# Two groups of loads change queues in a backward recurrence, and the weight-gradient stage loads one tile per transfer

## The chip, the cores and the metric

The kernel runs on one core of one Trainium2 chip. The metric is the time of one execution on the device in microseconds (us). The kernel before took 4817.9 us, the median of three runs (4813.3 to 4832.0 us).

A core has a tensor engine (PE; its weight loads are listed as PEld), a vector engine (DVE), a scalar engine (ACT), GpSimd (POOL) and SyncE (SP), which here does nothing but issue transfers. Each engine works through its own list of instructions in order and waits on semaphores. Transfers between the chip's memory (HBM) and the core's on-chip memory are issued by SyncE, GpSimd or ACT, each on a queue of its own.

## What is computed

A block of a model, forward and backward. `xn` is the layer norm of `x` (2048 rows of 640). Part A is a recurrent attention: the rows go through 64 segments of 32 in order, each joined with 8 memory rows that the segment before it left:

```python
for s in range(n_seg):
    h = concatenate([mem, xs])                 # 8 memory rows and 32 rows of the segment
    q, k, v = h @ Wq, h @ Wk, h @ Wv           # 32 heads of 128
    p = softmax(mask(q @ k.T * scale))
    o = (p @ v) @ Wo
    mem, out[s] = o[:8], o[8:]
```

Part B is a gated feed-forward layer, `g = silu(B(xn))`, and the result is `x + A(xn) * g`. The outputs are this result and the gradients of `x`, of the first memory and of all seven weights. So the 64 segments are gone through a second time, from last to first, with the gradient of the memory rows.

## The kernel before

The program runs in stages: layer norm and the feed-forward layer (0 to about 250 us), first projections, the forward recurrence (to about 1590 us), the rest of attention and the prologue of the backward pass (to 1819 us), the backward recurrence (to about 3086 us), the gradients of Wq, Wk, Wv (to about 4240 us), and the rest. In the two recurrences and the weight gradients the order in which each engine does its work is the order in which the code is written: `in_order` (line 283) chains each engine's instructions.

**Backward recurrence** (`phase4_Abwd`, lines 1105 to 1572). A step of `chain(t, gap)` handles one segment's memory rows. It projects the gradient with Wo (L316), copies the two halves out (DVE and ACT, L90 and L92), turns them (L324), forms the value gradients (`vgrad`, L1214), the probability gradients, and sends everything back through Wv, Wk and Wq (L335) to the gradient that the next step starts from (L344, L360, L1352). Into the gaps between these (`gap("W0")` to `gap("G6")`) fall the *units*: the 32 rows of three segments at a time (a tile `tl` of 96 rows and 24 memory rows), four heads at a time (`qd`). A step takes two or three. A unit is loaded (`ld`, L1358), turned (`turn`, L1388 and L1395; its turned values go to HBM as VTD), multiplied (`dprob`, L1405), put through the softmax's gradient (`dsoft`; stored as DSA), and closed by `gmem` (L1433), whose result `gks` goes to HBM as GXP. There are four buffers for loaded units; the load of a unit follows the `gmem` of the one that frees its buffer. `gks` has one buffer.

Besides the units' loads a step needs loads of its own for the step after it. `load_g(t)` (line 1196) brings what the riding value gradients need, the 32 ordinary rows of the segment that ride along in `vgrad`: the output gradients `xr` (256 KB, tile named `gor` in the profile), the probabilities `prf` (256 KB, from PRA, also `gor`) and the memory rows' probabilities `prm` (80 KB, from PMX). It is written right after the step's `vgrad`, whose operands it overwrites. `prx_copy` (line 1204) then arranges `prf` on GpSimd for the next step's `vgrad`. Other loads are `loads` (VTD, PM), `load_q`, `load_k` (KS and rows, L1227 to L1234) and `load_xp`.

All of these loads are issued by SyncE, but for one: the memory rows of queries and values of a unit (QVM, 48 KB, L1375), which GpSimd issues. GpSimd also issues the stores of VTD, DSA, GXP and the step's results (L351), and does the copies `lv`, `ride` and `prx`.

**Weight gradients** (`phase6_Awgrads`, line 1648). For each of eight groups of heads, 22 units go through turns and products (`s1` to `s4`, L1685 to L1760), and then 15 long accumulations `wg` (L1773) close the group. The first steps of the next group's first units (`head`) are written between the `wg` blocks. The class `Fetch` (line 1575) loads the units into six slots of the tile `land`, with five rows of data each: DSA, probabilities, output gradients, queries, keys. `to(u)` (line 1638) loads ahead up to unit `u`; in each group the first two units are loaded singly and the other twenty in pairs, two tiles in one transfer where the source allows it. For this PRA and DSA are single HBM tensors over all tiles. The memory rows of gradients and keys are loaded by GpSimd, tile by tile (`load_m`, L249), everything else by SyncE.

## Time and profile before

| | |
|---|---|
| median of the timed runs | 4817.9 us |
| the profiled execution | 4806.3 us (its span 4804.6 us) |
| granted PE clock over the span | 0.965 |
| PE busy | 4381.2 us, 91% |
| POOL, DVE, ACT busy | 2279.4, 2254.2, 1573.5 us |
| transfers | 858.4 MB, mean 179 GB/s |
| SyncE's queue (q1) | 568.2 MB |
| GpSimd's queue (q0) | 231.2 MB |
| ACT's wait for the landing of GXP at L1435 | 317.0 us |

The profile comes from one execution, so sums of its durations are set against that execution's own time. "Idle before" an instruction is time in which its engine had nothing to do; the profile names the event that ended it, where it finds one, and writes "issue" where it finds none. Issuing a transfer keeps GpSimd busy, and is listed for SyncE as `SPq`. Tiles are named by the buffer that they share, so `kT`, `oTm` and `vt` also stand for units' loads.

### The profile page before, as it was taken

To read this page: it belongs to the slowest core of one execution; us is meant where nothing else is said; L and a number is where in the kernel's file an instruction comes from. 1 tells how busy PE (TensorE), PEld (TensorE's weight loads), DVE (VectorE), ACT (ScalarE), POOL (GpSimd) and SP (SyncE) were. 2 spreads that over 40 slices of the span, in tenths; PEclk is the share of its full clock that TensorE was granted. 3 is DMA by queue.
4 is the path that set the end of the run, shared out by engine and by line. 5 is a ranking of instruction groups with operands and counts; after the bars stand their busy time and mean duration, and the time that the engine had idled before them with its cause. 6 is when DMAs were issued, how large, how long until landed. Compare 5 with 4: busy or idle time off the path is not lost. (4 is left out here: it accounts for less than half of the span.)

```text
span 4804.6 us, 164028 instructions
## 1 busy us (share of the span) xinstructions
PE 4381.2 (91%) x66656; PEld 2768.8 (58%) x66872; DVE 2254.2 (47%) x7188; ACT 1573.5 (33%) x4328; POOL 2279.4 (47%) x3830
## 2 busy tenths in 40 slices
PE   8998999999999887889889898889999999999999
PEld 4544555555555545655556565556655555667675
DVE  8735666666666444444444444334433333311460
ACT  5433555555444422333333333222222222200000
POOL 6532555565555324666666666533433333311340
PEclk9999999999999998999999989899999999999999
DMA  8773666566555786777777676676655556769783
GB/s 269 227 254 118 181 178 180 174 179 179 173 167 169 174 208 188 207 208 202 209 197 200 191 197 200 162 151 152 156 141 125 120 122 148 192 183 226 163 181 98
DMA packets 987532, 858.44 MB, mean 179 GB/s; under 512 B 509694, under 2 KB 851666, under 8 KB 984816
## 3 DMA queue, kind: packets, MB, share of 16 engines
q1 hardware_dynamic: 768807, 568.20, 44.9%
q0 software_dynamic: 135696, 231.22, 16.7%
q10 hardware_dynamic: 82275, 48.52, 3.9%
q8 instruction: 527, 8.63, 0.8%
q14 instruction: 227, 1.86, 0.1%
HBM read 501.77 MB, written 305.90 MB: 168 GB/s over the span
## 5 line engine op out<-in xcount | busy, mean ns | idle before, releaser
L1773 PE MATMUL wg<-gr,hr 128*128 128x512 bf16 x2352 | 519.1, 379 | 2.5
L1773 PEld LDWEIGHTS <-hr 128*128 128x128 bf16 x2400 | 233.9, 98 | 278.9
L316 PEld LDWEIGHTS <-hx 128*32 128x32 bf16 x10240 | 252.3, 98 | 245.5 <-issue 38.2
L1752 PE MATMUL g<-land,ghacc 128*128 128x320 bf16 x2048 | 328.8, 307 | 0.9 <-DVE ghacc L1756 0.8
L90 DVE CAST wgo<-wg 128x512 bf16<-128x512 f32 x72 | 49.8, 691 | 471.3 <-PE wg L1773 471.3
L902 POOL DMA_DIRECT2D OR<-xv x163 | 90.0, 552 | 360.7 <-ACT xv L92 331.2
L90 DVE CAST stg<-bank 128x512 bf16<-128x512 f32 x256 | 177.0, 691 | 159.2 <-PE bank L316 156.1
L1710 POOL DMA_DIRECT2D GSP<-grs x48 | 25.6, 546 | 452.9 <-ACT grs L1702 452.6
L1752 PEld LDWEIGHTS <-ghacc 128*128 128x128 bf16 x2048 | 194.3, 100 | 67.8 <-issue 0.9
L335 PE MATMUL bank<-WvT,gv 128*32 128x320 bf16 x4096 | 206.1, 353 | 4.2 <-issue 4.2
L1392 POOL DMA_DIRECT2D VTD<-gvT x176 | 130.2, 740 | 160.1 <-ACT gvT L1391 135.6
L834 ACT ACTIVATE xP<-xsp,xnm 120x120 bf16<-120x120 f32 (+1 forms) x540 | 186.1, 372 | 27.4 <-DVE xnm L816 27.4
L854 POOL TENSOR_TENSOR xP<-xP,xrz 120x480 bf16<-120x480 bf16 x163 | 161.4, 990 | 50.0 <-DVE xrz L853 38.3
L316 PE MATMUL bank<-WoT,hx 128*32 128x512 bf16 x2560 | 170.4, 418 | 11.9 <-DVE hx L1352 10.8
L92 ACT CAST wgo<-wg 128x512 bf16<-128x512 f32 x48 | 28.1, 585 | 466.0 <-PE wg L1773 407.6
L249 POOL DMA_DIRECT2D land<-GOS x256 | 145.9, 576 | 73.0 <-DMA land<-KS 16.2
L1695 PE MATMUL r6p<-land 120*128 120x128 bf16 (+1 forms) x1408 | 116.3, 223 | 70.3 <-DMA land<-QVM 19.5
L249 POOL DMA_DIRECT2D land<-KS x256 | 143.0, 565 | 67.1 <-DMA land<-KS 13.1
L1435 ACT ACTIVATE gks<-gkp 128x96 f32<-128x96 f32 (+1 forms) x176 | 44.4, 252 | 392.6 <-DMA GXP<-gks 317.0
L335 PE MATMUL bank<-Wo,oTm 128*32 128x320 bf16 x4032 | 155.1, 308 | 18.2 <-DVE oTm L705 18.2
L1340 POOL DMA_DIRECT2D DSA<-kT x256 | 156.4, 618 | 20.6 <-DVE xPT L1247 10.4
L92 ACT COPY ghacc<-t6g 128x384 bf16<-128x384 bf16 (+1 forms) x176 | 82.4, 468 | 253.2 <-PE t6g L1728 242.5
(394 smaller groups left out, 11055.3 us busy)
## 6 DMA issues: line engine op xcount, KB each, us to landing
QVS<-stg SPq DMA_DIRECT2D x128, 256.0 KB
kT<-VTD SPq DMA_DIRECT2D x64, 320.0 KB
PRA<-xP POOLq DMA_DIRECT2D x168, 120.0 KB
VTD<-gvT POOLq DMA_DIRECT2D x168, 120.0 KB
OR<-xv POOLq DMA_DIRECT2D x163, 120.0 KB
land<-DSA SPq DMA_DIRECT2D x80, 240.0 KB
land<-PRA SPq DMA_DIRECT2D x80, 240.0 KB
orr<-OR SPq DMA_DIRECT2D x14, 1280.0 KB
```

Source lines behind the costliest of these rows:

```text
L90: return nc.vector.tensor_copy(out, in_)
L92: return nc.scalar.copy(out, in_)
L249: eng.dma_start(d, src if src.shape[0] > 1 else src[0])
L316: k.nc.tensor.matmul(bank[32 * g:32 * g + 32, :], x[:, dc, :], W[:, dc, c0:c0 + 512], start=(dc == 0), stop=(dc == k.DC - 1), tile_positio ...
L335: k.nc.tensor.matmul(pm[p0:p0 + nq, 0:320], x[:, h, :], W[:, h, 320 * b:320 * b + 320], start=(first and i == 0), stop=(last and i == 15), ...
L834: nc.scalar.activation(Pb[0:n, j, 0:n], sp[0:n, j, :], ACT.Exp, bias=nmx[0:n, j:j + 1], scale=k.scale, accum_out=Z[0:n, j:j + 1])
L854: eng.tensor_tensor(Pb[0:n, :, 0:n], Pb[0:n, :, 0:n], bc_last(rz[0:n], n), ALU.mult)
L1340: nc.gpsimd.dma_start(k.DSR[tl][nx + 8 * s:nx + 8 * s + 8, 16 * a:16 * a + 16, d0:d0 + c1 - c0], dS[:, a, c0:c1])
L1392: nc.gpsimd.dma_start(k.VTD[tl][:, :, h0:h0 + 4, :], vTq[:])
L1695: nc.tensor.matmul(pr[:, j * P:(j + 1) * P], lh[0:n, j, :], rw[i][0:n, j * P:(j + 1) * P], start=True, stop=True)
L1752: nc.tensor.matmul(pg[:], ring[:, i, j, r0:r0 + P], Ws[qd][i][:, j, 320 * h:320 * h + 320], start=(i == 0 and j == 0), stop=(i == 1 and j ...
L1773: nc.tensor.matmul(pw[:], hr[:, tl, dc * P:(dc + 1) * P], grs[i][:, tl, :], start=(tl == 0), stop=(tl == NF - 1))
```

## The change

`load_g` issues its three transfers on GpSimd instead of SyncE. The memory rows of a unit's queries and values are issued by SyncE instead of GpSimd, but for the 19 units of the prologue. The weight-gradient stage loads every unit by itself; the slots of `land` are laid out unit by unit, and PRA and DSA are one HBM tensor for each tile again. Before that stage, three units are loaded ahead instead of four.

```diff
-        self.PRA = mk("PRA", (self.NR, H, P))
-        self.DSA = mk("DSA", (self.NR, H, P))
...
-            self.PR.append(self.PRA[120 * tl:120 * tl + n])
-            self.DSR.append(self.DSA[120 * tl:120 * tl + n])
+            self.PR.append(mk(f"PR{tl}", (n, H, P)))
+            self.DSR.append(mk(f"DSR{tl}", (n, H, P)))
...
         def load_g(t):
             tl, s = t // 3, t % 3
-            nc.sync.dma_start(xr, k.g_rows(t))
-            nc.sync.dma_start(prf, k.PR[tl][32 * s:32 * s + 32].rearrange("q (g h) c -> g q (h c)", g=4))
+            nc.gpsimd.dma_start(xr, k.g_rows(t))
+            nc.gpsimd.dma_start(prf, k.PR[tl][32 * s:32 * s + 32].rearrange("q (g h) c -> g q (h c)", g=4))
             v = k.PMX[t]
             v = bass.AP(tensor=v.tensor, offset=v.offset, ap=[[2560, 4], [320, 32], [1, 320]])
-            nc.sync.dma_start(prm[:].rearrange("p h c -> p (h c)"), v)
+            nc.gpsimd.dma_start(prm[:].rearrange("p h c -> p (h c)"), v)
...
-            nc.gpsimd.dma_start(
+            (nc.gpsimd if early else nc.sync).dma_start(
                 qv[nx:n], k.QVM[t0:t0 + ns, :, qd // 2, :, 512 * (qd % 2):512 * (qd % 2) + 512].rearrange("t r i c -> (t r) i c"))
...
-                    fetch[0].to(2 if g == "G1" else 4)
+                    fetch[0].to(2 if g == "G1" else 3)
...
-        land = [t[0:120, self.NB * 512 * j:self.NB * 512 * (j + 1)].rearrange("p (i c) -> p i c", c=512) for j in range(5)]
-        self.land = dict(zip("dpgqk", land))
+        b = [[t[0:120, 512 * (5 * i + j):512 * (5 * i + j) + 512] for i in range(self.NB)] for j in range(5)]
+        self.dS, self.P = [[four(x) for x in y] for y in b[0:2]]
+        self.rows = dict(zip("gqk", b[2:5]))
...
-    def ld(self, u, two):
+    def ld(self, u):
...
+        nc.sync.dma_start(dS[0:n], k.DSR[tl][:, h0:h0 + 4, :])
+        nc.sync.dma_start(Pr[0:n], k.PR[tl][:, h0:h0 + 4, :])
+        rw = []
+        for nm in ("g", "q", "k"):
+            r = self.rows[nm][u % self.NB]
+            src = k.g_src(tl, c0, c0 + 512) if nm == "g" else k.x_src(tl, nm, c0, c0 + 512)
+            k.load_x(r, 0, src, nc.sync)
+            if nm == "q":
+                t0, (ns, nm_, nx, n) = 3 * tl, k.geo(tl)
+                nc.sync.dma_start(r[nx:n], k.QVM[t0:t0 + ns, :, qd // 2, 0, 512 * (qd % 2):512 * (qd % 2) + 512].rearrange("t r c -> (t r) c"))
             else:
-                for i in range(m):
-                    k.load_m(self.land[w][:, i0 + i, :], tl + i, w, c0, c0 + 512, nc.gpsimd)
+                k.load_m(r, tl, nm, c0, c0 + 512, nc.gpsimd)
...
     def to(self, u):
-        u = min(u, len(self.units))
-        while self.n < u:
-            two = self.n % self.k.NTL > 1
-            if two and self.n + 2 > u:
-                break
-            self.ld(self.n, two)
-            self.n += 2 if two else 1
+        while self.n < min(u, len(self.units)):
+            self.ld(self.n)
+            self.n += 1
```

On the other engines (PE, DVE, ACT) the instructions and their order stay as they are.

More of the change, by code (lines that the diff above doesn't have):

```diff
@@ L1601, in ld @@
         c0, h0 = qd * 512, qd * 4
-        base = u % self.NB - u % 2
-        m = 2 if two else 1
-        i0 = base if two else base + 1 - u % 2
-        if two:
-            assert u % 2 == 0 and self.units[u + 1] == (qd, tl - 1)
-            tl -= 1
-        ns, nm, nx, n = k.geo(tl)
-        put = lambda w, p0, p1: self.land[w][p0:p1, i0:i0 + m, :]
-        for w, A in (("d", k.DSA), ("p", k.PRA)):
-            A = A[120 * tl:120 * tl + m * n, h0:h0 + 4, :]
-            nc.sync.dma_start(put(w, 0, n), A.rearrange("(i r) h c -> r i (h c)", i=m))
@@ L1613, in ld @@
-        for w in "gqk":
-            srcs = []
-            for i in range(m):
-                src = k.g_src(tl + i, c0, c0 + 512) if w == "g" else k.x_src(tl + i, w, c0, c0 + 512)
-                assert len(src) == 1
-                srcs.append(src[0][2])
-            if two and srcs[0].tensor is srcs[1].tensor:
-                v = srcs[0]
-                assert [list(p) for p in v.ap] == [list(p) for p in srcs[1].ap] and len(v.ap) == 2
-                v = bass.AP(tensor=v.tensor, offset=v.offset, ap=[list(v.ap[0]), [srcs[1].offset - v.offset, 2], list(v.ap[1])])
-                nc.sync.dma_start(put(w, 0, nx), v)
-            else:
-                for i, v in enumerate(srcs):
-                    nc.sync.dma_start(self.land[w][0:nx, i0 + i, :], v)
-            if w == "q":
-                nc.sync.dma_start(put(w, nx, n), k.QVM[3 * tl:3 * tl + m * ns, :, qd // 2, 0, 512 * (qd % 2):512 * (qd % 2) + 512]
-                                  .rearrange("(i t) r c -> (t r) i c", i=m))
-            else:
-                for i in range(m):
-                    k.load_m(self.land[w][:, i0 + i, :], tl + i, w, c0, c0 + 512, nc.gpsimd)
@@ L1633, in ld @@
-        four = lambda ap: ap.rearrange("p (h c) -> p h c", h=4)
-        for v in range(u, u + m):
-            i = v % self.NB + 1 - 2 * (v % 2)
-            self.st["l", v] = (four(self.land["d"][:, i]), four(self.land["p"][:, i]), [self.land[w][:, i] for w in "gqk"])
-    def to(self, u):
-        u = min(u, len(self.units))
-        while self.n < u:
-            two = self.n % self.k.NTL > 1
-            if two and self.n + 2 > u:
-                break
-            self.ld(self.n, two)
-            self.n += 2 if two else 1
+        n = k.geo(tl)[3]
@@ new lines, in ld @@
+        dS, Pr = self.dS[u % self.NB], self.P[u % self.NB]
+        nc.sync.dma_start(dS[0:n], k.DSR[tl][:, h0:h0 + 4, :])
[8 more added lines that the diff above has]
+                nc.sync.dma_start(r[nx:n], k.QVM[t0:t0 + ns, :, qd // 2, 0, 512 * (qd % 2):512 * (qd % 2) + 512].rearrange("t r c -> (t r) c"))
+            else:
+                k.load_m(r, tl, nm, c0, c0 + 512, nc.gpsimd)
+            rw.append(r)
@@ L1648, in phase6_Awgrads @@
+        self.st["l", u] = (dS, Pr, rw)
+    def to(self, u):
+        while self.n < min(u, len(self.units)):
+            self.ld(self.n)
+            self.n += 1
 def phase6_Awgrads(k, X, W0, fetch, out0, out3, out4, out5):
```

## The prediction

> **What bounds the kernel now.** The page's first table has the tensor engine (PE) busy for 91% of the span, so a change of queues can only give back idle PE time, or add to it. I first cut the span into stages by the first and last start of each stage's matmuls and asked for a table of windows. The change touches two stages: the backward recurrence (1819 to 3086 us) and the weight gradients (3086 to 4240 us).

> ```profile
> 1819.00:3086.00 1267.00, 1125.87 (x28400) 749.76 (x28403) 578.72 (x2872) 388.88 (x1156) 781.69 (x1438) 0.92 0.70 195
> 3086.00:4240.00 1154.00, 1054.33 (x8738) 667.43 (x8779) 405.61 (x893) 297.69 (x578) 418.35 (x743) 0.98 0.62 144
> ```

> Read the window, its length, busy time of PE, PE weight load, DVE, ACT and POOL, granted clock, DMA share and GB/s. The recurrence leaves PE idle (matmul and weight load both) for 138 us, and its clock is 0.92, that is, some 200 us at half speed. The weight-gradient stage leaves 98 us. Next the waits of the recurrence, an answer per engine (total us, times, longest):

> ```profile
> PEld L324 <- ACT gs L92: 54.3, 50, 3.7
> ...
> PEld L1388 <- issue: 41.7, 31, 4.1
> ```
> ```profile
> POOL prx L1207 <- DMA gor<-PRA: 90.0, 40, 13.6
> ```
> ```profile
> SPq L1227 <- DMA gor<-PRA: 96.7, 39, 3.3
> ```

> PE loses most at two places: L324, which needs ACT's copy of a projection, and L1388, the first transpose of a unit, which needs the unit's load ("issue" here means that the profile names no releaser; the landings below name it). GpSimd and SyncE both wait for `gor<-PRA`, one of the three transfers of `load_g`. One step's SyncE queue shows why:

> ```profile
> 2085.40 0.57 SPq L1198 DMA_DIRECT2D gor<-GX  x1
> 2086.07 0.56 SPq L1199 DMA_DIRECT2D gor<-PRA  x1
> 2086.72 0.52 SPq L1202 DMA_DIRECT2D prm<-PMX  x1
> 2087.33 0.95 SPq L275 DMA_DIRECT2D kT<-QVS  x1
> 2088.33 3.27 SPq L275 DMA_DIRECT2D kT<-GX  x1
> 2091.65 1.41 SPq L1379 DMA_DIRECT2D kT<-PRA  x1
> ...
> 2097.08 0.29 SPq L1227 DMA_DIRECT2D vt<-KS  x1
> ```
> ```profile
> 2099.71 0.23 PEld L1388 LDWEIGHTS <-kT 120*128 120x128 bf16 x4 [3.72 <-issue]
> ```

> Landings come from the trace's semaphore updates: a transfer's last update before the next issue on its semaphore. The three `load_g` transfers land 7.7, 10.5 and 10.9 us after issue (medians). While they run, their queue moves 2048-byte packets of 84 ns, only some four at a time: each is spread over four of the 16 DMA engines. Two 256 KB loads are 256 packets, 64 for each of four engines, 5.4 us, and PMX adds 1.0. Unit loads issued within 1.5 us behind them take 10.7 us (35 of them), others 3.8 us (115). Here `kT<-QVS` is issued at 2087.33 and lands at 2099.61, and PE starts 0.1 us later.

> The other loss is a longer chain. `prx_copy` blocks GpSimd until `gor<-PRA` has landed; behind it on GpSimd is the store `GXP<-gks`; ACT may not write `gks` again until that store has landed; and behind that on ACT is the copy that L324 needs:

> ```profile
> 2064.20 0.25 ACT L1435 ACTIVATE gks<-gkp 128x96 f32<-128x96 f32 x1 [6.24 <-DMA GXP<-gks]
> 2064.35 0.58 ACT L92 CAST gs<-bank 128x512 bf16<-128x512 f32 x1
> ```

> **load_g on GpSimd's queue.** SyncE loses 192 issues of about 0.55 us, 1.65 us per step, and GpSimd gains 192. On GpSimd they stand behind the stores that end the previous step: it comes free at a median of 4.4 us after the step's value-gradient matmuls begin, where SyncE issued at 2.6. So the last two start about 2 to 3 us later. Queued behind are the `lv` copy (needed each fourth step), a VTD store that waits 2 us for ACT anyway, and the first GXP store.

> [...]

> What it gives: L1388. Over 15 stalls both halves of PE stand idle 35 us. Cold clock follows stalls: over the 58 steps with units, step length fits 14.2 us + 0.81 x idle + 0.39 x half-clock time + terms for units. Fifteen clock drops of 4.9 us x 0.39 are 28 us. Of these 63 us I count 50: the load at 3.8 to 6 us leaves 3 us to spare before its transpose. If cover fails the term is zero; it is not below zero, since SyncE's queue only gets shorter.

> L324: 50 stalls, 49 us, of which about 23 us is ACT's copy itself (0.4 to 0.6 us each in undisturbed steps); 26 us are the chain. GpSimd reaches `prx_copy` at 12.8 us, now starts it at 14.4; with a landing at 11 to 12 us, 1.5 us come back. Bounds: 26 us plus as much for the clock, or nothing; I take 20.

> Entry: before the first step PE waits 7.3 us for `gor<-GX` and 3.5 us for `prx`, with `load_g` behind eight other issues on SyncE. GpSimd is free from 1820.6 us. I count 7.

> Price: eight semaphores serve GpSimd's transfers in turn, so the eighth issue after each `load_g` transfer waits until that has landed: the second of the four small DSA stores, some 5 us later. At 6 us of landing that is 0 to 1 us per step: +15 in 64 steps, the bounds being 0 and the rival below.

> **Units' memory rows on SyncE's queue.** 157 transfers of 48 KB, 2.45 per step: GpSimd gets back 2.45 x 0.63 = 1.5 us per step, which cancels the three it gains; SyncE pays about 1.4. They also stop standing behind GXP on GpSimd: in the step above they were issued at 2092.50, landed at 2097.76, and by themselves would have held PE past 2096. I count zero, since it is a condition of the 50 us; between -5 and +5.

> **Weight gradients, one tile per transfer.** SyncE goes from 576 transfers to 1056, with the same bytes in the same 1 KB rows. PE's stalls lie here:

> ```profile
> 3541.97 0.38 PE L1685 MATMUL t<-ident,land 120*128 120x120 bf16 x4 [1.41 <-DMA land<-DSA]
> ...
> 3544.99 0.38 PE L1695 MATMUL r6p<-land 120*128 120x128 bf16 x4 [0.99 <-DMA land<-GOS]
> ...
> 3546.41 0.38 PE L1695 MATMUL r6p<-land 120*128 120x128 bf16 x4 [1.03 <-DMA land<-QVM]
> ```

> They come after each long block of `wg` matmuls. A pair loads only once both slots are free, so units 4 and 5 of the next head group are issued after `wg`; one by one, unit 4 fits before it. About 3 us in seven groups is 21 us.

> [...] The rows: under full load (DMA share 1.08) pairs land after 7 us and single tiles already in this stage after 6, because they queue, and issues follow each other at 0.45 us: six are 2.7 us, against 3.5 us per unit. [...] I take +10 (bounds 0 and +120, near the row), so -11 for this part.

> **Sum.** -50 - 20 - 7 + 15 - 11 = -73 us. The profiled execution took 4806.3 us (span 4804.6), 0.2% under the median 4817.9 of the three timed runs. From the median: 4745 us.

> **Rivals.** (a) Slower: on GpSimd the three transfers again share four engines and land after 10.5 us or more. They start 2 to 3 us later, so `prx_copy` starts near 16.6 us, 2.2 us later than now, and the GXP store, ACT and L324 with it: 60 x 2.2 x 0.81 = +107, less the 50 that SyncE's shorter queue gives: +57, 4875 us. It decides once the landing exceeds about 8 us. For it: GpSimd has some 14 us of issues and copies in a 20 us step. [...] (c) The move does nothing: the unit loads stay slow because they share engines with the same bytes, and the sum is the entry and noise: 4810 us.

> **Chances.** Forecast 0.66; (a) 0.15; (b) 0.10; (c) 0.09. The forecast's own terms (50 down to 25, 20 up to 50, clock) span 4695 to 4785. To leave out no more than two in ten the range goes from 4690 to 4822, which takes in (b) and (c) and leaves (a). Faster by over 0.5% (below 4794; about what a measurement of this kernel can tell from no change) 0.70, within 0.5% 0.14, slower 0.16.

> **What would show it.** Right: the waits for `gor<-PRA` on SyncE gone, L1388's idle below 10 us, unit loads near 4 us throughout, the recurrence's clock above 0.94 and its length near 1205 us; the stalls after `wg` gone. Wrong: GpSimd waiting over 100 us at L1207 or at L1340 for `load_g`, ACT's `gks` waits above 317 us, or SyncE never catching up between two `wg` blocks. What breaks the forecast is a landing of `load_g` on GpSimd of over 8 us.

## The result, and the profile after

The changed kernel takes 4795.6 us (median of 11 runs), the kernel before 4816.2 us (median of 11): ratio 0.9958, 95% interval 0.994 to 0.9976. The forecast was 4745. Faster, but by 0.4% and not by 1.5%; whether one calls that a gain or no change is a matter of the bound. The profiled execution took 4788.9 us (span 4787.1), 17.4 us less than the one before.

The table of windows shows where. Both kernels are cut at the same places: first projection with Wo, first matmul of the weight gradients, last `wg`. Before:

```profile
1819.00:3090.00 1271.00, 1128.86 (x28480) 751.70 (x28479) 580.00 (x2877) 389.72 (x1158) 784.69 (x1444) 0.92 0.70 195
3090.00:4236.00 1146.00, 1047.93 (x8624) 663.00 (x8672) 403.84 (x889) 296.85 (x576) 414.33 (x736) 0.98 0.62 144
```

After:

```profile
1814.00:3105.00 1291.00, 1139.09 (x28479) 752.05 (x28478) 578.03 (x2876) 391.44 (x1158) 818.79 (x1477) 0.92 0.76 192
3105.00:4218.00 1113.00, 1043.44 (x8624) 658.57 (x8672) 407.65 (x888) 293.80 (x576) 416.07 (x740) 0.98 0.55 149
```

With the borders to a tenth of a microsecond, the backward recurrence takes 1291.5 us (1271.1 before: **+20.4**, forecast -62), the weight gradients 1112.6 (1145.3 before: **-32.7**, forecast -11). The clock of the recurrence is still 0.92. Of its 20 us, 10 are idle time of PE (138 to 148 us) and 10 are PE being busy longer for the same instructions (1128.9 to 1139.1); the reason for the second part was not followed up. The rest of the kernel differs by 5 us, all of it ahead of the recurrence, and this says little: in e1 below, whose code there is nearly that of the changed kernel, the recurrence starts 10 us later than in it.

Next PE's waits in the recurrence (total us, times, longest). The two lines of the kernel before that grow (L335 and L360, now L333 and L358), in its list of weight loads:

```profile
PEld L360 <- DVE fsum L344: 22.0, 48, 1.2
PEld L335 <- issue: 14.8, 26, 2.4
```

The changed kernel, weight loads and then matmuls:

```profile
PEld L333 <- issue: 64.6, 42, 4.1
PEld L358 <- DVE fsum L342: 53.0, 63, 4.5
```
```profile
PE bank L358 <- DVE fsum L342: 39.0, 29, 4.3
PE bank L333 <- issue: 38.4, 28, 2.8
...
PE bank L322 <- ACT gs L92: 8.2, 11, 2.4
```

The two lines that led the list before (L324, now L322, and L1388, now L1386) have fallen as forecast: the first transposes wait 2 us in place of 36, L322 waits 12 in place of 53. (These and all sums below count only time in which both halves of PE stand idle.) In their place stand two others. L358, the turn of a step's folded result, waits 42 us where it waited 13. And PE stops for 64 us (stops of over 0.25 us) for "nothing that the profile shows", where it stopped for 7: 32 of 38 times at L333, the projections back through Wv, Wk and Wq.

GpSimd did come to `prx_copy` earlier, and its data was there. GpSimd's waits in the same stretch:

```profile
POOL DSR L1338 <- DMA gor<-GOS: 36.4, 21, 4.8
POOL DSR L1338 <- DMA gor<-PR: 21.3, 24, 2.4
POOL prx L1205 <- DMA gor<-PR: 18.2, 5, 7.0
```

The wait at `prx_copy` is 18 us (90 before). The first two lines, with 11 us for `gor<-GX`, are the price that the forecast named: GpSimd's semaphores (eight, which its issues take in turn), 69 us of its time. The three transfers land 8.2 to 8.6 us after issue (medians), and not after 6.

**What stops L333.** Here is PE's part of the timeline around one stop:

```profile
2160.96 2.21 PE L333 MATMUL bank<-WqT,gqT 128*8 128x320 bf16 x59
2165.45 0.43 PE L333 MATMUL bank<-WqT,gqT 128*8 128x320 bf16 x5 [2.29 <-issue]
```

PE stops for 2.29 us within a row of 64 equal matmuls that need nothing from any other engine; no instruction at the stop carries a wait. So I numbered PE's instructions in the order of their starts. All 38 stops in the recurrence are at a number that leaves 25 when divided by 256. In every other trace of this case all such stops, or all but one, share one remainder too (some records can be missing from a trace, so it need not be 25). This points to the list of instructions itself, and the page's table of DMA queues has it:

```profile
## 3 DMA queue, kind: packets, MB, share of 16 engines
...
q8 instruction: 528, 8.65, 0.8%
```

These are packets of 16 KB. In the recurrence before, 223 of them (3.65 MB) stand against 56,959 PE instructions: 64 bytes each, 256 to a packet. In the changed kernel PE stops at 38 of 224 borders between such blocks. A packet begins a median 1.2 us after PE has entered the block before it, takes 1.1 us, and PE goes on 1.3 us after its end at the earliest: 3.6 us in sum. The blocks ahead of the stops, in which PE has little to wait for, last 4.5 us without the stop (median). Ahead of the stops, the packet began 3.5 us after that moment (median), and PE went on 1.5 us after its end. In the stop above it started at 2162.32 and ended at 2163.90. So what is late is the start of a packet; what it stands behind the trace does not say.

The traces tie this to `load_g`. Where PE enters a block 3 to 7 us after the first issue of `load_g`, the packet for the next block begins a median 3.2 us later, and 25 of the 38 stops follow (49 borders); at the other 175 borders it begins after 1.2 us. Two more kernels below have `load_g` in this form on GpSimd, and there it is 3.1 and 1.2 us (e7), 3.0 and 1.35 us (e11). With `load_g` on SyncE there is no such place: 1.2 and 1.2 us before, 1.2 and 1.1 in e1, 1.0 and 1.1 in e2.

### The profile page after: what moved, and what is told of

It reads as the page before. It is cut to its first block, busy times and chain, and to the rows that moved or that the text cites. A ratio compares the mean times of both kernels' runs of the same rounds, so it can differ in the third digit from the quotient of the medians.

```text
span 4787.1 us, 164773 instructions
## 1 busy us (share of the span) xinstructions
PE 4384.3 (92%) x66656; PEld 2763.6 (58%) x66872; DVE 2256.2 (47%) x7188; ACT 1573.0 (33%) x4328; POOL 2314.0 (48%) x3865
## 5 line engine op out<-in xcount | busy, mean ns | idle before, releaser
L1338 POOL DMA_DIRECT2D DSR<-kT x256 | 156.1, 615 | 79.3 <-DMA gor<-GOS 36.4
L333 PE MATMUL bank<-WqT,gqT 128*8 128x320 bf16 x4096 | 165.9, 311 | 28.9 <-issue 28.6
L314 PE MATMUL bank<-WoT,hx 128*32 128x512 bf16 x2560 | 180.0, 436 | 11.7 <-DVE hx L1350 11.3
L333 PE MATMUL bank<-WvT,gv 128*32 128x320 bf16 x4096 | 187.8, 331 | 0.5 <-issue 0.5
L92 ACT CAST wgo<-wg 128x512 bf16<-128x512 f32 x48 | 28.1, 586 | 464.9 <-PE wg L1749 393.9
L333 PE MATMUL bank<-WkT,kT 128*8 128x320 bf16 x4096 | 168.7, 306 | 11.0 <-issue 9.3
L92 ACT COPY ghacc<-t6g 128x384 bf16<-128x384 bf16 (+1 forms) x176 | 82.6, 469 | 272.9 <-PE t6g L1704 266.2
L333 PE MATMUL bank<-Wo,oTm 128*32 128x320 bf16 x4032 | 153.9, 306 | 18.3 <-DVE oTm L703 18.3
```

The costliest lines, as they stand in the source:

```text
L92: return nc.scalar.copy(out, in_)
L314: k.nc.tensor.matmul(bank[32 * g:32 * g + 32, :], x[:, dc, :], W[:, dc, c0:c0 + 512], start=(dc == 0), stop=(dc == k.DC - 1), tile_positio ...
L333: k.nc.tensor.matmul(pm[p0:p0 + nq, 0:320], x[:, h, :], W[:, h, 320 * b:320 * b + 320], start=(first and i == 0), stop=(last and i == 15), ...
L1338: nc.gpsimd.dma_start(k.DSR[tl][nx + 8 * s:nx + 8 * s + 8, 16 * a:16 * a + 16, d0:d0 + c1 - c0], dS[:, a, c0:c1])
```

## The experiments

Two theories were put against each other. **Fetch**: the bursts of `load_g`, when GpSimd issues them, delay the packets with PE's instructions, and when SyncE issues them they do not. **Queue**: the GXP stores now stand behind `load_g` on GpSimd; ACT waits longer for them before it can write `gks`, and ACT's copy for L358 stands behind that. "Border" in the table means the stops of the first kind, "unit" the stalls at a unit's transposes; all are PE idle time in the recurrence, in us, from the profiled execution. "engines each" is for the two large transfers of `load_g` (the 80 KB from PMX stay on four): in the traces such a transfer ends with 4 updates of its semaphore on SyncE's queue in e1 and on ACT's in e3, and with 16 on SyncE's in e16. On GpSimd's queue in the changed kernel every transfer has 16 updates (of those of `load_g`'s first, a median 4 come in its last 1.5 us), so for the kernels with `load_g` on GpSimd the column has what the same shape shows on SyncE. From 2 to 8 us after the first issue of `load_g`, GpSimd's queue there has a median of 5 packets of 4096 bytes in flight (179 ns each); SyncE's before had 4 of 2048 bytes (84 ns each). On which engines they run no trace says. "rows" is the queue of the units' memory rows, "gks" the number of its buffers. All but "before" have the single tiles. e5, e6 and e8 have no row; their numbers stand in the text.

| kernel | load_g on | engines each | rows | gks | recurrence | border | L358 | L322 | unit | ratio (95%) |
|---|---|---|---|---|---|---|---|---|---|---|
| before | SyncE | 4 | GpSimd | 1 | 1271.1 | 7 | 13 | 53 | 36 | |
| after | GpSimd | 4 | SyncE | 1 | 1291.5 | 64 | 42 | 12 | 2 | 0.9958 (0.994-0.9976) |
| e1 | SyncE | 4 | GpSimd | 1 | 1277.3 | 3 | 14 | 54 | 39 | 0.9923 (0.9905-0.994) |
| e2 | SyncE | 4 | SyncE | 1 | 1313.3 | 4 | 13 | 71 | 49 | 0.9993 (0.9974-1.0012) |
| e3 | ACT | 4 | SyncE | 1 | 1361.2 | 14 | 15 | 20 | 35 | 1.0095 (1.0075-1.0114) |
| e7 | GpSimd | 4 | GpSimd | 1 | 1338.8 | 61 | 57 | 7 | 29 | 1.0052 (1.0034-1.007) |
| e9 | SyncE, order | 4 | GpSimd | 1 | 1257.9 | 10 | 13 | 41 | 37 | 0.9875 (0.9853-0.9897) |
| e10 | SyncE, order and place | 4 | GpSimd | 1 | 1286.8 | 9 | 15 | 79 | 6 | 0.9933 (0.9914-0.9953) |
| e11 | GpSimd | 4 | SyncE | 2 | 1250.5 | 88 | 13 | 4 | 0 | 0.9909 (0.9889-0.9928) |
| e12 | GpSimd | 16 | SyncE | 1 | 1295.4 | 13 | 99 | 14 | 0 | 0.9955 (0.9936-0.9974) |
| e13 | GpSimd | 16 | SyncE | 2 | 1186.4 | 25 | 14 | 18 | 1 | 0.9725 (0.97-0.9749) |
| e14 | as e10 | 4 | GpSimd | 2 | 1259.1 | 8 | 14 | 16 | 50 | 0.9891 (0.987-0.9913) |
| e15 | as e9 | 4 | GpSimd | 2 | 1237.6 | 12 | 13 | 12 | 45 | 0.9839 (0.9813-0.9866) |
| e16 | SyncE | 16 | SyncE | 2 | 1208.5 | 8 | 14 | 4 | 36 | 0.977 (0.9757-0.9783) |

### The parts of the change, each alone

**e1**, the changed kernel with both queues as before:

```diff
-            nc.gpsimd.dma_start(xr, k.g_rows(t))
+            nc.sync.dma_start(xr, k.g_rows(t))
...
-            (nc.gpsimd if early else nc.sync).dma_start(
+            nc.gpsimd.dma_start(
```

> Only the weight-gradient part of the change; load_g on SyncE and the memory rows on GpSimd, as before. In the changed kernel the weight gradients took 1112.6 us against 1145.3, the backward recurrence 1291.5 against 1271.1. If the two parts add up, this run keeps the -33 and loses the +20: about 4773 us, ratio 0.993, recurrence 1271, weight gradients 1113. If single tiles were paid for somewhere else (the first theory of the sum: +10 for smaller transfers), it is 4790 or more.

It took 4784.0 us. The weight gradients take 1116.7 us: the weight-gradient part alone brings more than the whole change does, and the two moves of queues together cost about 0.35% on top of it. This part is three things at once (one transfer per tile, slots laid out unit by unit, one HBM tensor per tile); which of them brings the gain was not tested.

**e2**, only `load_g` back on SyncE:

> The changed kernel with load_g back on SyncE; the memory rows stay on SyncE. [...] Theory 'queue': the +20 come from the GXP stores standing behind load_g on GpSimd (L358 waiting for ACT's copy 42 us against 13); that one also goes back here, but the stalls without a wait stay near 54 us, since something else in the change makes them.

It took 4817.8 us, 34 more than e1. The border stops are gone (4 us, 64 in the changed kernel), which speaks for "fetch"; but the memory rows, now behind `load_g` on SyncE, hold the units up. PE's waits (weight loads) in its recurrence:

```profile
PEld L322 <- ACT gs L92: 72.3, 48, 4.3
...
PEld L1386 <- DMA kT<-QVM: 39.8, 14, 4.4
```

**e7**, only the memory rows back on GpSimd:

> The changed kernel with the units' memory rows back on GpSimd (load_g stays there too). e2 against e1 shows that the memory rows on SyncE cost some 33 us while load_g is on SyncE as well. Theory 'they stood behind load_g there': with load_g gone from SyncE it makes no difference which queue they use but for their place: now they stand behind load_g on GpSimd, a unit's first transpose waits for them again (20 to 40 us at L1386 with the clock behind it), and the time is 4800 to 4825. Rival 'SyncE's 157 more issues are what cost': the time falls by 20 to 30 to about 4765. The stalls of PE's instruction packets stay near 54 us in either case.

It took 4849.1 us, more than expected. The same transfers now stand behind `load_g` on the other queue, and units wait for them again. The same view:

```profile
PEld L333 <- issue: 70.5, 43, 5.6
PEld L358 <- DVE fsum L342: 70.3, 61, 6.1
...
PEld L1386 <- DMA kT<-QVM: 30.6, 11, 6.4
```

So the two moves belong together as long as `load_g` has its four-engine form: in the recurrence `load_g`'s alone costs 62 us (e7 against e1), the rows' alone 36 (e2 against e1), both 14. In both kernels what shares a queue with `load_g` pays. The border stops are 61 us here and 64 in the changed kernel, the two kernels with `load_g` on GpSimd, and 3 to 4 in e1 and e2.

**e3**, `load_g` on ACT:

> The changed kernel with load_g issued by ACT. Theory 'fetch': from ACT the three transfers are confined to four engines, as from SyncE, so PE's instruction packets come in time (stalls without a wait at L333 under 12 us, against 54), and SyncE's queue is still free of load_g (stalls at the first transpose under 5 us); recurrence about 1225, time 4710 to 4740. Theory 'queue': GXP no longer stands behind load_g, L358's wait for ACT falls from 42 to about 13 us, but the stalls at L333 stay near 54 us: recurrence about 1260, time 4755. Against both: ACT waits for the end of vgrad before it can issue, and issues for some 0.5 us each (up to 64 x 2 us = 130 us of ACT's time, on the chain only where ACT is late).

It took 4867.7 us: far from both. The border stops are down to 14 us, as "fetch" had it, and L358 to 15, as "queue" had it. What neither counted are ACT's waits at its next copies (total us, times, longest):

```profile
ACT gv L92 <- DMA kT<-QVM: 45.8, 7, 9.8
...
ACT gv L92 <- DMA gor<-PR: 38.6, 9, 7.1
ACT gv L92 <- DMA xP<-PR: 34.3, 5, 9.5
```

ACT's issue waits for transfers that SyncE issued (QVM, xP): in this trace the transfers of both report to the same eight semaphores. ACT's copies stand behind, and PE waits 87 us for them at L333.

### The two theories, one cause at a time

**e5 and e6** add bursts that nobody waits for to e1, which has few border stops:

```diff
+        def extra_copies(t):
+            for i in range(2):
+                nc.gpsimd.dma_start(k.XT[t, i], k.g_rows(t))
...
                 load_g(t - 1)
+                extra_copies(t - 1)
```

This is e5: the 256 KB of `load_g`'s output gradients go to spare HBM twice per step, in the shape that they have in `load_g`. In e6 the source is `k.g_rows(t).rearrange("g q c -> q g c")`, and `XT` has that shape.

> [...] Theory 'fetch': PE's instruction packets are held up by such bursts whatever they carry: stalls without a wait, at the same place modulo 256 instructions, go from 4 us in e1 to 30 to 60 us, most of them at L333, and the recurrence from 1277 to 1310 or more. Theory 'order on the queue': the stalls without a wait stay under 12 us, and what is lost shows as waits (GpSimd's semaphores, GXP, L322 and L358).

> As e5, the same bytes in the same 2 KB rows, but with the 32 rows as slowest dimension, so that each extra transfer is spread over all 16 engines (a quarter of the burst on each). Theory 'fetch by long bursts on one engine': stalls without a wait under half of e5's, below 20 us. Rival 'it is the bytes in total': as many as in e5. The issues on GpSimd and the waits for its semaphores are the same in both, so the difference of e5 and e6 is the price of the four-engine shape.

e5 took 5005.2 us (ratio 1.0377, 1.0353 to 1.04), e6 4854.4 (1.0065, 1.0041 to 1.0088). The shape of the same bytes is worth 150 us; with slowest dimension 4 (e5) the recurrence takes 1492.7 us, with 32 (e6) 1352.3. But the border stops are 18 and 9 us, under what "fetch" expected of e5, and most of e5's loss is elsewhere: 79 us at units' transposes, 103 at L323 (L322), 53 at L359 (L358). In e5's trace the packets are hardly late either: where PE enters a block 3 to 7 us after the first extra issue, they begin after a median 1.0 us, against 3.2 in the changed kernel. So "whatever they carry" is not borne out: these bursts, which go to HBM and not to the core's memory, delay PE's program far less than `load_g` does, and why was not tested. What e5 and e6 show is what the shape with slowest dimension 4 costs everything else, 140 us of the recurrence.

**e12** is the direct one: `load_g` stays on GpSimd and only changes its shape.

```diff
-            nc.gpsimd.dma_start(xr, k.g_rows(t))
-            nc.gpsimd.dma_start(prf, k.PR[tl][32 * s:32 * s + 32].rearrange("q (g h) c -> g q (h c)", g=4))
+            gr = k.g_rows(t)
+            pq = k.PR[tl][32 * s:32 * s + 32].rearrange("q (g h) c -> g q (h c)", g=4)
+            pd = prf
+            for g in range(4):
+                nc.gpsimd.dma_start(xr[32 * g:32 * g + 32], gr[g])
+            for g in range(4):
+                nc.gpsimd.dma_start(pd[32 * g:32 * g + 32].rearrange("p h c -> p (h c)")[:, 0:pq.shape[2]], pq[g])
```

> The changed kernel with load_g still on GpSimd, but its two large transfers cut into four each, one for 32 rows, so that each is spread over all 16 engines: the same bytes and rows, without a burst of 64 KB on one engine. Theory 'fetch by bursts': the stalls at the borders of instruction blocks fall from 64 us to under 20. Rival 'it is GpSimd's queue as such, or the bytes': they stay above 40. Six more issues of 0.7 us per step on GpSimd and its eight semaphores cost on top (up to +100 us), so the time itself may be worse than 4789; the count of border stalls is what tells.

PE's waits (weight loads):

```profile
PEld L358 <- DVE fsum L342: 110.5, 63, 8.4
...
PEld L333 <- issue: 19.6, 21, 3.9
```

The border stops fall from 64 to 13 us, with the same queue and the same bytes: for `load_g`, "fetch by bursts" holds. (e12 also spreads the bytes over more time, in eight issues 0.7 us apart instead of two; which of the two spreads does it was not tested apart.) The time, 4805.7 us, does not fall: L358 waits 99 us. With six more issues per step on GpSimd, ACT's wait for the GXP stores has grown. The changed kernel:

```profile
ACT gks L1433 <- DMA GXP<-gks: 265.0, 83, 8.9
```

And e12:

```profile
ACT gks L1438 <- DMA GXP<-gks: 353.0, 96, 11.6
```

**e11** takes away the other cause, with two buffers for `gks` (there was no room for a second one, so the small tile `Dx` moved into spare columns):

```diff
-            ks = fl.tile([P, ns, 4, 8], F32, name="gks", tag="gks")
+            ks = fl.tile([P, ns, 4, 8], F32, name="gks", tag="gks", bufs=2)
```

> The changed kernel with two buffers for gks (Dx moved into spare columns to make room). Theory 'queue': ACT's waits for GXP (262 us) nearly vanish, and with them the wait of L358 for ACT's copy (42 us, 13 in the kernel before); the stalls at the instruction blocks' borders (64 us) stay. Time 4789 to about 4750. If L358's wait stays at 40 us, it came from something else, such as the border stalls at L333, which delay the projection that ACT copies.

The same view:

```profile
PEld L333 <- issue: 102.5, 58, 5.2
...
PEld L358 <- DVE fsum L342: 24.1, 62, 1.3
```

L358 is back at 13 us, and ACT's wait for GXP, 265 us, falls to 1 us: "queue" holds too. The recurrence takes 1250.5 us, 41 less than in the changed kernel, about what was expected. That 4782.8 us come out where 4750 were expected lies outside it: in the profiled execution the stages ahead of the recurrence take 16 us more than in the changed kernel's and those behind the weight gradients 11 us more, for a reason that was not followed up. The border stops grow from 64 to 88 us, 54 stops against 38: with less to wait for in between, PE comes to more borders ahead of their packets. Each cause hid part of the other.

**e13** is both at once:

> e12 with the two gks buffers of e11: load_g on GpSimd, spread over 16 engines, and no GXP chain. e12 has taken the border stalls from 64 to 13 us and shows 99 us at L358; e11 has taken L358's 42 to 13. If the two are all that stood between the change and the forecast, both go at once: PE idle in the recurrence 157 to about 70 us, recurrence 1295 to about 1215 (the forecast had 1205), time about 4715. If GpSimd's 6 more issues per step are the limit, another wait takes their place (L333 or L358 for GpSimd or ACT, 50 us or more) and the time stays above 4760.

Its recurrence in the table of windows:

```profile
1821.00:3008.00 1187.00, 1097.05 (x28486) 737.32 (x28486) 580.07 (x2878) 390.81 (x1157) 980.61 (x1862) 0.96 0.78 208
```

It took 4691.8 us, ratio 0.9725 (0.97 to 0.9749): faster than both kernels by far. PE's idle time in the recurrence falls from 149 us in the changed kernel to 87, the clock rises from 0.92 to 0.96, and the stage takes 1186 us, under the forecast's 1205. Units' loads on SyncE now land within 5.3 us nine times in ten (their slowest kinds within 10.8 in the kernel before), and `load_g` after 3.8 to 5.4 us (medians). GpSimd, the feared limit, is busy for 981 us and has room for it.

**e16**, the same on SyncE's queue:

> e13 with the nine transfers of load_g on SyncE: the same shape (16 engines each), the same two gks buffers, only the queue is that of before. e13 took 4691.8 us. Theory 'the shape is what counts': on SyncE, too, the transfers land soon and nothing behind them is held for 10 us; SyncE pays 6 more issues of 0.55 us per step, units' loads start 3 us later; stalls at the first transpose under 20 us, time 4690 to 4715. Rival 'the queue counts': the units' loads behind nine transfers are late again, 30 us or more at L1392, time 4735 or more, so the move to GpSimd is needed for the gain.

It took 4713.2 us. Most of the gain comes without `load_g` on GpSimd: with the single tiles, the shape and the second buffer. The queue's own share is the difference to e13, 0.45%. It lies in the stalls at units' transposes, 36 us against 1, of the size that the rival named, though not because loads are held: the units' loads land as soon as in e13 (within 4.9 us nine times in ten), but they are issued later. SyncE's issues fill 960 us of the stage (614 in e13), and the load of a unit's queries and values is issued a median 3.4 us after the last `gmem` before it (0.4 in e13). The border stops are fewer (8 against 25).

### Without the move: order and place on SyncE

**e8, e9, e10** start from e1. e9 issues the probabilities first in `load_g`; e10 also writes `load_g` behind the units' loads of gap G1; e8 does the latter with the old order and moves `prx_copy` to the end of the step.

> The kernel of e1 (load_g and the memory rows on the queues of before, so no bursts from GpSimd) with load_g written after the units' loads of gap G1 instead of before them, and prx_copy moved behind the GXP stores of gaps G3 and G5 on GpSimd. If the two stalls that the change was costed at are real and can be had without the bursts: L1386's 37 us fall under 10, L322's 49 to about 25, stalls without a wait stay under 12, recurrence 1277 to about 1215, time 4715 to 4730. If the loads are slow because of the bytes and not of their place behind load_g, L1386's stalls stay, and the time is 4770 or more; if prx becomes late, PE waits for it at L1212.

> The kernel of e1 with load_g's second transfer (the probabilities, which prx_copy needs) issued ahead of the first. It lands about 2 us earlier, GpSimd's wait at prx_copy (90 us before) nearly goes, and the GXP store behind it, ACT's gks and ACT's copy for L322 come earlier. By the prediction's term for this chain (26 us of idle and as much for the clock, 20 counted): recurrence 1277 to 1250 to 1260, time 4760 to 4770, L322 <- ACT from 49.5 to about 25 us. If the chain does not hold PE (ACT's copy is late for another reason), 4780 to 4790. L1386's 37 us stay in either case.

> As e9, and load_g written after the units' loads of gap G1, as in e8; prx_copy stays where it was. In e8 the units' first transposes no longer waited (1 us against 37), but PE waited 112 us for prx_copy, moved too far back. Here its data should land 12 us after vgrad's start (4.9 + 7.1), before GpSimd reaches it at 12.8. So both stalls go without bursts from GpSimd: PE idle in the recurrence 136 to about 75 us, recurrence about 1205, time 4700 to 4725. If it is 4770 or more, the stalls of the units' loads were worth less than the prediction had it.

e8 took 4856.3 us (ratio 1.007, 1.0051 to 1.0089): the first transposes wait 2 us, but `prx_copy` came too late. PE's waits, matmuls:

```profile
PE bank L1212 <- POOL prx L1206: 121.9, 48, 12.7
```

e9 took 4765.7 us, as expected, with two lines swapped: the recurrence is 19 us shorter than e1's, about the 20 that the prediction had for the chain through `prx_copy`, GXP and `gks`, though L322's idle time falls by 13 only (54 to 41). e10 took 4795.7 (0.9933, 0.9914 to 0.9953), not 4700 to 4725: the units' stalls are 6 us, but L322's grew to 79: ACT still waits for GXP (272 us).

**e14** and **e15** are e10 and e9 with two `gks` buffers.

> e10 (load_g on SyncE behind the units' loads, probabilities first) with two gks buffers. In e10 L1386's stalls went and L322 <- ACT grew to 72 us, with ACT waiting 272 us for GXP. Without that wait L322 falls to 25 us or less, PE idle 142 to about 90 us, recurrence 1287 to about 1225, time about 4735. If L322's wait stays, it isn't the GXP chain, and the time is 4780 or more.

> e9 (load_g on SyncE, probabilities first) with two gks buffers: L322 <- ACT 37 to about 12 us, L1386's 35 us stay, border stalls stay under 20: recurrence 1258 to about 1230, time about 4738. Against e14 it prices load_g's place: if the stalls at L1386 are worth 50 us as the prediction had it, e14 is faster than this by 30 or more.

e14 took 4770.1 us (0.9891, 0.987 to 0.9913), e15 4746.6 (0.9839, 0.9813 to 0.9866). L322 falls to 16 and 12, so its wait was the GXP chain. The comparison was to price the units' stalls by `load_g`'s place, and can't: they are back, 50 us in e14 and 45 in e15. In e15 the units' loads behind `load_g` are slow (the four kinds from QVS, QVX, GX and GOS within 9.4 to 10.1 us nine times in ten). In e14 they land within 5.3 us and are late all the same, a median 3.0 us after the last `gmem` before them. SyncE itself is held there: some 175 us of its waits, before it can issue the loads behind, end with a landing of `load_g`. So a four-engine `load_g` on SyncE seems to cost the units in both places, once by slow landings and once by late issues.

## Why the prediction was wrong

The direction was right, the size wrong by a factor of more than three, and by a wrong division: the part expected to carry the gain lost 20 us, the part expected to do little gained 33. The moves of queues made the recurrence slower; that the direction came out right rests on the other part, and is luck.

- **Units' loads, -50.** The stalls went as forecast, 36 to 2 us, though the loads are not "near 4 us throughout": by kind, nine in ten land within 5.0 to 8.8 us. The clock's share (28 of the 63 us it was taken from) did not come: other stops took the place of these, and the clock stayed at 0.92 (195 us at half clock before, 198 after).
- **L324, -20.** Its idle time fell by 41 us, more than forecast. But the GXP stores behind `load_g` on GpSimd became slower at the long end (9 in 10 within 7.8 us, before 6.3; the median 3.8 is even lower). ACT's wait for them is shorter in sum (265 us, before 289) but has longer single waits (8.9 us, before 6.2), and 28 of these us came back at L358. The chain moved by one link; the prediction had followed it only to L324. Net -12.
- **Entry, -7.** Measured: 10.8 us to 5.8, that is -5.
- **Price of GpSimd's semaphores, +15.** No run shows the landing of `load_g` after 6 us that this term takes: in the changed kernel the three land 8.2 to 8.6 us after issue, cut into pieces in e13 after 3.8 to 5.4. In the changed kernel the probabilities land 11.2 us after the step's value gradients begin, 14.0 before. The semaphores cost GpSimd 69 us, about 1 us per step, the upper end of the estimate. What of this reaches PE is part of the 28 at L358.
- **Memory rows, 0.** Right only beside the other move: without it they cost 36 us (e2), with it they save 47 (the changed kernel against e7, both in the recurrence).
- **The step that failed**: the move was counted as relief for SyncE's loads, with GpSimd's semaphores as its only price. The three no longer held SyncE's loads, but with them on GpSimd PE's own program came late: +57 us of border stops (7 to 64), a term that the prediction put at nothing. With the others (-34 units, -12 for L324 and L358, -5 entry) this gives about +6 of idle time; +10 were measured. The prediction looked for who else waits in `load_g`'s queue, and not for what else could come late while it runs. The 6.8 us of stops in the trace before, and the queue of 16 KB packets on its page, were there to be seen. By the prediction's own words a landing of over 8 us breaks the forecast, through a later `prx_copy`; this is not how it broke, since the wait at `prx_copy` fell from 90 to 18 us, so rival (a) did not come about.
- **Weight gradients, -11.** The stalls in the some 12 us after `wg` fell from 20.6 to 6.8 us: 13.8 of the 21 counted, though some have only moved back (in the 20 us after `wg` they fell from 24.7 to 14.6). The term that was mis-sized is the price of smaller transfers, +10. None shows, and no run shows the +120 us that it was bounded by: the loads land after a median 3.7 us, before 6.5, and the DMA share of the stage falls from 0.62 to 0.55 for the same data. The stalls in the rest of the stage fall as well, from 75 to 62. What remains waits for the first of a unit's loads, as PE's waits in this stage of the changed kernel show:

```profile
PEld L1661 <- DMA land<-DSR: 58.0, 62, 3.1
```

The stage has 1550 loads in place of 1081 and is 32.7 us shorter. `load_g`'s shape, with the second `gks` buffer, counted for more than its queue: with `load_g` on SyncE e16 still has a ratio of 0.977, against 0.9725 for e13.

Not settled: the theory of the border stops rests on their place in PE's list, on the late start of the packets 3 to 7 us after `load_g`'s issue, on the kernels with and without `load_g` on GpSimd, and on e12. The trace does not say on which of the 16 engines a packet runs, so that `load_g`'s packets stand directly ahead of it was not seen, and e5, whose bursts have the same shape and queue, does not show late packets. Why border stops still come in e13 (25 us) was not followed up.

## What to carry to other kernels

When a load moves to another queue, ask how many DMA engines its shape uses, and what else comes late while it runs. Here two transfers of 256 KB on four engines each held up the loads behind them on SyncE's queue (10.7 us to land in place of 3.8), and from GpSimd they came with 64 us of late instructions on PE; cut into pieces that end with 16 updates in place of 4 (e16), and with a second buffer, they were worth more than the choice of queue (0.977 on SyncE, 0.9725 on GpSimd). All 38 PE stops without a wait (of over 0.25 us) in the changed kernel's recurrence were at the same place modulo 256 instructions, and the packet ahead of them began after 3.5 us in place of 1.2: with such stops, look at the instruction queue's packets. Two causes that feed the same engine can hide each other: e11 and e12 took one away each, for 0.9909 and 0.9955, and only e13, without both, showed the gain.
